# A fused cosine attention and mixer kernel: output of both heads in one tile, one pair transposed on TensorE, token and channel steps reordered

## The chip, the cores and the metric

The kernel runs on one core of one Trainium2 chip. The metric is device time in microseconds (us), the median over runs. The profile is one more execution of the same program; its times are counted from the start of its span.

## The reference

Eight batches, twelve heads, 448 positions, 64 columns a head. The attention normalizes the rows of q and k, divides the scores by tau = 0.1, and applies a softmax. Its output, heads side by side, is the input x of a mixer with a token product over positions and a channel product over columns:

```python
q_n = q / (norm(q) + 1e-06); k_n = k / (norm(k) + 1e-06)
attn = softmax(q_n @ k_n.T / tau)
x = (attn @ v)                      # [8, 448, 768]
h = relu(x.T @ w_tok1) @ w_tok2     # 448 -> 256 -> 448
u = x + h.T
out = u + relu(u @ w_ch1) @ w_ch2   # 768 -> 1536 -> 768
```

## The kernel before

**Pairs.** Two heads make a pair; six pairs make a batch, 48 pairs in all (i = 0 to 47). Work is written out pair by pair in an order fixed by hand: each engine executes its instructions in the order of the program, and waits on the others through semaphores. A "slot" is the stretch that begins with the scores of pair i and also does other steps of earlier and later pairs.

**Steps of a pair.** `load_qk` and `load_v` load it by DMA (issued by SP). `square` (L239 on ACT, L241 on POOL) and `sums` (L264, a reduction on VectorE) give the squared norms; `norms` turns them into factors by Ln and Exp on ACT (L277, L278) and a sum and a reciprocal on VectorE (L274, L275); `scale` (L293, mostly POOL) writes the normalized rows kq as fp16. They are then transposed into qk: by TensorE and a copy on VectorE (`tpose`, L317 and L319) for pairs below `DMA_T0` = 12, by a DMA transpose on SP (`tpose_dma`, L325) from there on. `score(i, c)` (L340) makes a piece of the transposed scores for both heads and ACT takes its exponential into pt (L341). There are four pieces in pairs 0 to 11; from pair 12 on (`old` is false) there are three and a rest (`score_rest`, L347), over 128 rows instead of 112. `pv(i, hh)` (L379) multiplies pt by v with a column of ones, for one head, and VectorE divides by that column (L382, L383), which gives x. `cast_v` is POOL's copy of v.

**Mixer.** `tok1` (L392) and its ReLU on VectorE (rt, L395), `tok2` (L406) and the addition that gives u (L409), both per pair. u is transposed into ut by DMA (`udma`, L415) or on TensorE (`upose`, L421). When a batch is whole, `refill` queues its channel work as units: `m_ch1` (psG, L431, ReLU on ACT L434), twelve a batch; `m_ch2` (psF, L446, addition L450), two of 384 columns for each block of 128 rows, with the output DMAs after the second. `unit` takes the next one from the queue, and `due` decides by a running account how many go into a slot.

**PSUM.** Two pools: `ps` (tag "b") with two tiles of one bank, `ps2` (tag "s") with three tiles of two banks. A new tile of a tag takes the buffer of the tile two (three) before it and waits until that has been read. In the slots of pairs 1 to 5 before the change, "b" goes in turn to the output of head 0, the transposes, the output of head 1 and `warm` (matmuls on the identity that keep TensorE busy, L331); "s" goes to two score pieces, tok1, two score pieces, tok2.

**Order.** Pairs 1 to 5 have one hand-written slot, pair 6 another, in one loop (L560 to L619). From pair 7 on the loop at L649 is used, with `side(i)` for the work on POOL, ACT and SP. After pair 47 the last token steps and the remaining units follow (L681 to L692).

Of the kernel before, what the change touches and what calls it, by code (L numbers as in the profile page):

```python
# [7 lines left out]
FP32 = mybir.dt.float32  # L8
FP16 = mybir.dt.float16
# [13 lines left out]
def kernel(  # L23
# [21 lines left out]
    CT = C // 128  # L45
    TT = T // 128
    DH = 384
    NDH = D // DH
    NPAIR = H // 2
    NP_ALL = B * NPAIR  # L50
    HP = 3
    NHALF = 2 * B
    inv_tau = 1.0 / float(tau)
    EPS_NORM = 1e-6
    DMA_T0 = 12
    OLD = 2 * NPAIR
    SINGLE = 3 * NPAIR

# [306 lines left out]
    def pv(i, hh):  # L365
# [10 lines left out]
        for m, lo in enumerate(windows(i // NPAIR)):  # L376
            for c in range(nch):
# [5 lines left out]
        nc.vector.tensor_tensor(out=st["x"][:, :, hh * E:(hh + 1) * E], in0=psO[:, :, 0:E],  # L383
                                in1=_bcast_free(rec[:], E), op=ALU.mult)

    def tok1(i, wide=False):
        st = pipe[i]
        w1 = (0, 1, 2, 3) if (i // NPAIR) % 2 == 0 else (4, 0, 1, 2)
        psR = (ps2 if wide else ps).tile([128, TT, 128], FP32, name=f"psR_{i}", tag="s" if wide else "b")
        for tt in range(TT):  # L390
            for m in range(4):
                nc.tensor.matmul(psR[:, tt], w1t[:, w1[m], tt * 128:(tt + 1) * 128], st["x"][:, m],  # L392
                                 start=(m == 0), stop=(m == 3))
        st["rt"] = att.tile([128, TT, 128], FP16, name=f"rt_{i}", tag="rt", bufs=2)
        nc.vector.tensor_scalar_max(out=st["rt"][:], in0=psR[:], scalar1=0.0)  # L395
# [39 lines left out]

    ost = {}

    def m_ch2(b, m, dh, wide):
        gt = gts[b // 2]
        lo = 384 if m == 3 else 128 * m + (b % 2) * 512  # L440
        if dh == 0:
            ost[0] = outp.tile([128, D], FP32, name=f"ost_{b}_{m}", tag="ost")
        o = ost[0]
        psF = (ps2 if wide else ps).tile([128, 512], FP32, name=f"psF_{b}_{m}_{dh}", tag="s" if wide else "b")
        for ct in range(CT):
            nc.tensor.matmul(psF[:, 0:DH], gt[:, ct, lo:lo + 128], wc2t[:, ct, dh * DH:(dh + 1) * DH],  # L446
                             start=(ct == 0), stop=(ct == CT - 1))

        def add(p0, p1, bb, slot):
            nc.vector.tensor_tensor(out=o[p0:p1, dh * DH:(dh + 1) * DH].rearrange("p (j e) -> p j e", j=3),  # L450
                                    in0=psF[p0:p1, 0:DH].rearrange("p (j e) -> p j e", j=3),
                                    in1=u16[bb][p0:p1, 3 * dh:3 * dh + 3, slot], op=ALU.add)

        if m < 3:
            add(0, 128, b, m + b % 2)
        else:
            add(0, 64, b - 1, 3)
            add(64, 128, b, 0)
        if dh == 0:
            return  # L460
        if m < 3:
            r = 0
            for c, p0, p1 in pieces(*MAIN[m]):
                nc.sync.dma_start(out=out[b].rearrange("(p c) d -> c p d", c=NCH)[c, p0:p1], in_=o[r:r + p1 - p0])
                r += p1 - p0
        else:
            (c, p0, p1), = pieces(384, S)
            for bb, r in ((b - 1, 0), (b, 64)):
                nc.sync.dma_start(out=out[bb].rearrange("(p c) d -> c p d", c=NCH)[c, p0:p1], in_=o[r:r + 64])

    def ns(cols, n=1):
        return n * (cols / 2.4 + 2.5)
# [2 lines left out]
        return [(ns(S, DT), lambda wide, ct=ct: m_ch1(b, ct, wide)) for ct in range(CT)]  # L475

    def ch2_units(b):
        return [(ns(DH, CT), lambda wide, m=m, dh=dh: m_ch2(b, m, dh, wide))
                for m in ((3, 0, 1, 2) if b == B - 1 else range(3 + b % 2)) for dh in range(NDH)]

    queue = []
    fed = [0.0, 0.0]
# [20 lines left out]
    with tc.manual_schedule():  # L503
# [53 lines left out]
        load_v(4)  # L557
        load_qk(6)

        for i in range(1, NPAIR + 1):  # L560
            b, pj = i // NPAIR, i % NPAIR
            if i < NPAIR:
                if i == 1:
                    scale(2, 0)
                    scale(2, 1, nc.vector)
                else:
                    scaled(i + 1)
                    if i != 3:
                        weights_ch1(max(i - 3, 0))
                load_qk(i + 6)  # L570
                score(i, 0)
                score(i, 1)
                sums(i + 2)
                norms(i + 2, i + 3)
                if i >= 2:
                    tok1(i - 2, wide=True)
                pv(i - 1, 0)
                norms(i + 2, i + 3, dve=True)
                cast_v(i)
                square(i + 3, 0)  # L580
                if i == 1:
                    warm(10)
                tpose(i + 1)
                score(i, 2)
                score(i, 3)
                if i >= 2:
                    tok2(i - 2, pe=True, wide=True)
                pv(i - 1, 1)
                warm(8)
                square(i + 3, 1, act=True)  # L590
                if i == 1:
                    place_w2()
                load_v(i + 4)
                if 2 <= i < NPAIR - 1:
                    udma(i - 2)
                continue
            load_qk(12)
            scaled(7)
            score(i, 0)
            score(i, 1)  # L600
            score(i, 2)
            sums(8)
            norms(8, 9)
            pv(i - 1, 0)
            pv(i - 1, 1)
            norms(8, 9, dve=True)
            cast_v(i)
            load_v(i + 4)
            squares(9)
            scaled(8)  # L610
            weights_ch1(3)
            upose(i - 3)
            tok1(i - 2, wide=True)
            score(i, 3)
            tpose(i + 1)
            tok2(i - 2, pe=True)
            tok1(i - 1, wide=True)
            tok2(i - 1, pe=True)
            sums(9)  # L619

# [26 lines left out]
        for i in range(NPAIR + 1, NP_ALL):  # L649
            b, pj = i // NPAIR, i % NPAIR  # L650
            for c in range(KC):
                score(i, c)
            pv_rest(i - 1)
            pv(i - 1, 0)
            pv(i - 1, 1)
            if i == NPAIR + 1:
                upose(NPAIR - 2)
                upose(NPAIR - 1)
                refill(0)
            elif pj == 2 and b > 1:  # L660
                refill(b - 1)
            side(i)
            fed[0] += fed[1]
            unit(True)
            if old(i):
                score(i, KC)
            else:
                score_rest(i)
            if i > NPAIR + 1:
                tok2(i - 2)  # L670
            if i + 1 < DMA_T0:
                tpose(i + 1)
            if due():
                unit(True)
            while due():
                unit()
            tok1(i - 1)
            if i + 2 < SINGLE:
                for t in SU_AT.get(i, [i + 3]):
                    sums(t)  # L680
        last = NP_ALL - 1  # L681
        pv_rest(last)
        pv(last, 0)
        pv(last, 1)
        tok2(last - 1)
        unit()
        tok1(last)
        unit()
        tok2(last)
        refill(B - 1)  # L690
        while queue:
# [36 lines left out]
```

## Time and profile before

| What | Value |
|---|---|
| median of 5 runs | 397.64 us (396.24 to 398.49) |
| the profiled execution | 397.75 us, its span 396.0 us |
| TensorE busy | 376.0 us (95%), granted clock 0.988 on average |
| ACT, POOL, DVE busy | 224.7, 236.1, 210.7 us |
| slots 2 to 5 (pairs 2 to 5), first score to first score | 4.60, 4.36, 4.30, 4.18 us |
| slot 6 | 6.82 us (37.22 to 44.04) |
| slot 12 | 8.40 us (78.33 to 86.73) |
| DMA of weights, wc2t, second half | issued at 66.5 us, lands 10.8 us later |
| last units of the loop to the last batch's channel stage | 342.86 to 361.59 us |

PE is TensorE's matmul stream and PEld its weight loads, DVE is VectorE, SP issues DMAs. A matmul's row ends later than the next one starts, because matmuls are pipelined; on the chain of work that ended last they are cut to what they add. The granted clock is the share of full speed that TensorE was allowed.

### The profile page before, as it was taken

The numbers are of one execution on the slowest core, as the hardware profiler recorded it, in microseconds if no ns is written. First come the engines' busy times: TensorE is split into PE (matmuls) and PEld (weight loads), VectorE is DVE, ScalarE is ACT, GpSimd is POOL, SyncE is SP. The second block draws the span as 40 slices with busy tenths as digits, with TensorE's granted clock in tenths as the row PEclk, the third lists the DMA queues.
The fourth block names the chain that finished last, engine by engine and source line by source line (L and its number), as shares of the span: only waits on it lengthen the run. The fifth ranks groups of instructions, "written<-read, shape, count | busy, mean of one in ns | idle before, by whom it ended". The sixth has DMA issues, their size and how long they took to land.

```text
span 396.0 us, 10211 instructions
## 1 busy us (share of the span) xinstructions
PE 376.0 (95%) x4132; PEld 243.4 (61%) x4132; DVE 210.7 (53%) x469; ACT 224.7 (57%) x378; POOL 236.1 (60%) x383
## 2 busy tenths in 40 slices
PE   5799799799999999999999999999999999999994
PEld 5567566466656666666666666667656666655562
DVE  6889767557545565366444574465544553331031
ACT  5899578655665456764684447764674546511400
POOL 6899887888779392948678492939585540000000
PEclk8999999989999999999999999999999999999998
DMA  8999999997896689876997788695796394023022
GB/s 206 243 232 213 235 266 193 217 228 174 166 228 147 175 204 216 159 164 148 195 209 165 165 213 215 139 181 120 203 204 130 75 174 68 15 56 91 0 81 81
DMA packets 117951, 65.26 MB, mean 165 GB/s; under 512 B 75920, under 2 KB 114320, under 8 KB 117904
## 3 DMA queue, kind: packets, MB, share of 16 engines
q1 hardware_dynamic: 113104, 58.71, 68.6%
q0 software_dynamic: 4080, 5.21, 7.6%
q10 hardware_dynamic: 720, 0.69, 0.7%
q8 instruction: 32, 0.52, 0.6%
q14 instruction: 15, 0.12, 0.1%
HBM read 43.45 MB, written 11.01 MB: 138 GB/s over the span
## 4 chain that ended last, share of the span: by engine, by line
PE 81%; ACT 4%; DMA 4%; DVE 4%; POOL 4%; issue 2%; POOLq 0%
PE psF L446 28%; PE psG L431 25%; PE psO L379 9%; PE psS L340 6%; PE psU L406 5%; PE psR L392 4%; ACT pt L341 3%; DMA w2n<-in_moe_w_tok_dram 2%; DMA qk<-kq 2%; PE psQ L347 2%; POOL kq L293 2%; PE psO L362 1%; DVE ssq L264 1%; POOL w1t L182 1%; DVE ost L450 1%
## 5 line engine op out<-in xcount | busy, mean ns | idle before, releaser
L341 ACT ACTIVATE pt<-psS 128x896 f16<-128x896 f32 (+1 forms) x156 | 132.5, 917 | 58.4 <-PE psS L340 58.0
L431 PE MATMUL psG<-ut,wc1t 128*128 128x448 f16 x576 | 116.8, 352 | 0.8 <-ACT gt L434 0.8
L446 PE MATMUL psF<-wc2t,gt 128*128 128x384 f16 x672 | 117.1, 328 | 0.2 <-ACT gt L434 0.2
L446 PEld LDWEIGHTS <-gt 128*128 128x128 f16 x672 | 64.0, 98 | 40.0 <-issue 1.7
L434 ACT ACTIVATE gt<-psG 128x448 f16<-128x448 f32 x96 | 51.3, 543 | 60.9 <-PE psG L431 60.9
L293 POOL TENSOR_TENSOR kq<-kf,rn 128x384 f16<-128x384 f32 (+1 forms) x47 | 42.3, 900 | 72.6 <-ACT rn L281 62.0
L431 PEld LDWEIGHTS <-wc1t 128*128 128x128 f16 x576 | 53.8, 98 | 45.4 <-issue 1.1
L450 DVE TENSOR_TENSOR ost<-psF,u 128x384 f32<-128x384 f32 (+1 forms) x64 | 35.5, 555 | 65.2 <-PE psF L446 63.8
L264 DVE TENSOR_REDUCE ssq<-sq 128x15 f32<-128x960 f32 (+2 forms) x49 | 55.7, 1140 | 3.2 <-ACT sq L239 3.1
L395 DVE TENSOR_SCALAR rt<-psR 128x256 f16<-128x256 f32 x48 | 20.2, 420 | 62.6 <-PE psR L392 62.5
L293 POOL TENSOR_TENSOR kq<-qf,rn 112x512 f16<-112x512 f32 x45 | 47.0, 1044 | 3.0
L379 PE MATMUL psO<-vt,pt 128*128 128x65 f16 (+1 forms) x1248 | 48.7, 194 | 0.0
L379 PEld LDWEIGHTS <-pt 128*128 128x128 f16 (+1 forms) x1248 | 42.6, 98 | 5.1 <-issue 1.9
L340 PE MATMUL psS<-qk 64*128 64x448 f16 x312 | 41.2, 358 | 3.6 <-DMA qk<-kq 2.4
L383 DVE TENSOR_TENSOR x<-psO,rec 128x256 f16<-128x256 f32 x96 | 40.8, 425 | 3.3
L241 POOL TENSOR_TENSOR sq<-kf 128x384 f32<-128x384 f32 (+1 forms) x46 | 40.1, 873 | 1.9 <-DVE ssq L264 1.8
L241 POOL TENSOR_TENSOR sq<-qf 112x512 f32<-112x512 f32 x39 | 40.5, 1039 | 0.0
L409 DVE TENSOR_TENSOR u<-psU,x 128x512 f16<-128x512 f32 x48 | 33.0, 687 | 6.0 <-PE psU L406 4.4
L382 DVE RECIPROCAL rec<-psO 128x4 f32<-128x4 f32 x96 | 16.9, 176 | 29.8 <-PE psO L379 29.8
L406 PEld LDWEIGHTS <-w2t 128*128 128x128 f16 x384 | 24.6, 98 | 10.5 <-issue 3.3
L406 PE MATMUL psU<-rt,w2t 128*128 128x128 f16 x384 | 29.4, 219 | 1.7 <-DVE rt L395 1.1
L348 ACT ACTIVATE pt<-psQ 128x448 f16<-128x448 f32 x36 | 19.4, 539 | 18.6 <-PE psQ L347 18.6
(55 smaller groups left out, 266.7 us busy)
## 6 DMA issues: line engine op xcount, KB each, us to landing
qf<-in_q_dram SPq DMA_DIRECT2D x48, 224.0 KB, 3.9
kf<-in_k_dram SPq DMA_DIRECT2D x36, 192.0 KB, 3.5
vf<-in_v_dram SPq DMA_DIRECT2D x36, 192.0 KB, 3.2
vf<-in_v_dram SPq DMA_DIRECT2D x12, 224.0 KB, 8.7
out_dram<-ost SPq DMA_DIRECT2D x8, 336.0 KB, 3.2
wc1t<-in_moe_w_ch_dram POOLq DMA_DIRECT2D x4, 576.0 KB, 10.6
wc2t<-in_moe_w_ch_dram POOLq DMA_DIRECT2D x2, 1152.0 KB, 11.5
out_dram<-ost SPq DMA_DIRECT2D x8, 288.0 KB, 3.0
```

Source lines behind the costliest of these rows:

```text
L241: nc.gpsimd.tensor_mul(out=dst, in0=src, in1=src)
L264: nc.vector.tensor_reduce(out=h["ssq"][0:n, col, sl], in_=pipe[i]["sq"][0:n, sl], axis=AXX.X, op=ALU.add)
L293: eng.tensor_tensor(out=kq[0:p, a, 0:n].rearrange("p c g e -> p g c e"), in0=st["kq"[a]][:].rearrange("p (g c) e -> p g c e", g=2), in1=_b ...
L340: nc.tensor.matmul(psS[:, hh, 0:S], qk[hb, c * n:c * n + 128], qm[hb], start=True, stop=True)
L341: nc.scalar.activation(out=pts[i % 2][0:n, 2 * S * c:2 * S * (c + 1)].rearrange("p (h s) -> p h s", h=2), in_=psS[0:n, :, 0:S], func=AF.Ex ...
L379: nc.tensor.matmul(psO[:, m, 0:E + 1], pts[i % 2][0:n, at:at + 128], vt[0:n, i % HP, nch * hh + c, 0:E + 1], start=(old(i) and c == 0), st ...
L383: nc.vector.tensor_tensor(out=st["x"][:, :, hh * E:(hh + 1) * E], in0=psO[:, :, 0:E], in1=_bcast_free(rec[:], E), op=ALU.mult)
L406: nc.tensor.matmul(psU[:, m], w2t[:, tt, lo:lo + 128], st["rt"][:, tt], start=(tt == 0), stop=(tt == TT - 1))
L431: nc.tensor.matmul(psG[:, 0:S], wc1t[:, dt, ct * 128:(ct + 1) * 128], ut[b][:, dt].rearrange("p m s -> p (m s)")[:, lo:lo + S], start=(dt ...
L434: nc.scalar.activation(out=gt[:, ct, (b % 2) * S:(b % 2 + 1) * S], in_=psG[:, 0:S], func=AF.Relu)
L446: nc.tensor.matmul(psF[:, 0:DH], gt[:, ct, lo:lo + 128], wc2t[:, ct, dh * DH:(dh + 1) * DH], start=(ct == 0), stop=(ct == CT - 1))
L450: nc.vector.tensor_tensor(out=o[p0:p1, dh * DH:(dh + 1) * DH].rearrange("p (j e) -> p j e", j=3), in0=psF[p0:p1, 0:DH].rearrange("p (j e) ...
```

## The change

1. A new `pv_wide(i)` replaces `pv(i, 0)` and `pv(i, 1)` for pairs 0 to 5. It writes both heads into one two-bank tile of `ps2` and normalizes them with one reciprocal and one product. It stands behind scores 0 and 1, in place of head 0's product there and head 1's behind tok2.
2. In slots 2 to 5, tok1 and tok2 use `ps`, and tok1 stands ahead of `sums` and `norms`.
3. Slot 6 gets the same order; its scores 2 and 3 stand behind the transposes of pair 7. Its second tok2 (pair 5) goes behind the first three score pieces of slot 7.
4. `DMA_T0` is 13: pair 12 is transposed by `tpose` in slot 11.
5. After the last pair, five channel units are placed ahead of and between its steps, where two were placed before.
6. The last block of rows (batch 7, m = 2) is computed in 384, 256 and 128 columns. Its first 640 columns are stored once they are done, its last 128 by two DMAs of which ACT issues one.

```diff
-    DMA_T0 = 12
+    DMA_T0 = 13
...
+    def pv_wide(i):
+        st = pipe[i]
+        vt = vts[(i // HP) % NV]
+        st["x"] = att.tile([128, 4, 128], FP16, name=f"x_{i}", tag="x", bufs=3)
+        psO = ps2.tile([128, 2, 512], FP32, name=f"psO_{i}", tag="s")
+        o = psO[:, :, 0:4 * (E + 2)].rearrange("p h (m e) -> p h m e", m=4)
+        for hh in range(2):
+            for m, lo in enumerate(windows(i // NPAIR)):
+                for c in range(NCH):
+                    at = (2 * c + hh) * S + lo
+                    nc.tensor.matmul(o[:, hh, m, 0:E + 1], pts[i % 2][0:SC, at:at + 128],
+                                     vt[0:SC, i % HP, NCH * hh + c, 0:E + 1], start=(c == 0), stop=(c == NCH - 1))
+        rec = att.tile([128, 2, 4], FP32, name=f"rec_{i}", tag="rec2", bufs=2)
+        nc.vector.reciprocal(out=rec[:], in_=o[:, :, :, E])
+        nc.vector.tensor_tensor(out=st["x"][:].rearrange("p m (h e) -> p h m e", h=2), in0=o[:, :, :, 0:E],
+                                in1=_bcast_free(rec[:], E), op=ALU.mult)
...
         if m < 3:
             r = 0
-            for c, p0, p1 in pieces(*MAIN[m]):
-                nc.sync.dma_start(out=out[b].rearrange("(p c) d -> c p d", c=NCH)[c, p0:p1], in_=o[r:r + p1 - p0])
+            for n, (c, p0, p1) in enumerate(pieces(*MAIN[m])):
+                eng = nc.scalar if st and n == 0 else nc.sync
+                eng.dma_start(out=out[b].rearrange("(p c) d -> c p d", c=NCH)[c, p0:p1, st:hi],
+                              in_=o[r:r + p1 - p0, st:hi])
                 r += p1 - p0
...
+        cuts = ((0, DH, None), (DH, D, 0))
+        ends = ((0, DH, None), (DH, D - 128, 0), (D - 128, D, D - 128))
...
-                score(i, 0)
-                score(i, 1)
-                sums(i + 2)
-                norms(i + 2, i + 3)
-                if i >= 2:
-                    tok1(i - 2, wide=True)
-                pv(i - 1, 0)
-                norms(i + 2, i + 3, dve=True)
...
-                if i >= 2:
-                    tok2(i - 2, pe=True, wide=True)
-                pv(i - 1, 1)
-                warm(8)
...
+            score(i, 0)
+            score(i, 1)
+            if i >= 2:
+                tok1(i - 2)
+            sums(i + 2)
+            norms(i + 2, i + 3)
+            pv_wide(i - 1)
+            norms(i + 2, i + 3, dve=True)
...
+            tpose(i + 1)
             score(i, 2)
+            score(i, 3)
+            if i >= 2:
+                tok2(i - 2, pe=True)
+            warm(8)
...
-            upose(i - 3)
-            tok1(i - 2, wide=True)
-            score(i, 3)
-            tpose(i + 1)
-            tok2(i - 2, pe=True)
-            tok1(i - 1, wide=True)
-            tok2(i - 1, pe=True)
-            sums(9)
+        upose(i - 3)
+        tpose(i + 1)
+        score(i, 2)
+        score(i, 3)
+        tok2(i - 2, pe=True)
+        tok1(i - 1)
+        sums(i + 3)
...
             for c in range(KC):
                 score(i, c)
+            if i == NPAIR + 1:
+                tok2(i - 2, pe=True)
             pv_rest(i - 1)
...
         last = NP_ALL - 1
+        unit()
         pv_rest(last)
         pv(last, 0)
         pv(last, 1)
+        unit(True)
         tok2(last - 1)
-        unit()
+        unit(True)
         tok1(last)
-        unit()
+        unit(True)
+        unit(True)
         tok2(last)
         refill(B - 1)
```

## The prediction

> **What bounds the kernel now.** I read the chain that ended last first: it is 81% TensorE, so time lost or won counts where TensorE stands still, or where another engine paces it. Then I took windows over the stages and the timelines of the four places that the diff touches. Below, "slot i" is the stretch that starts with the scores of pair i; its start is the first L340 matmul.
>
> From the page and the windows (columns: busy time and count of PE, PEld, DVE, ACT, POOL; granted clock; DMA share; GB/s):
>
> ```profile
> PE 81%; ACT 4%; DMA 4%; DVE 4%; POOL 4%; issue 2%; POOLq 0%
> 20.00:37.20 17.20, 16.43 (x288) 12.36 (x284) 15.44 (x39) 16.87 (x30) 17.20 (x21) 1.00 1.19 221
> 37.20:44.00 6.80, 5.08 (x86) 3.90 (x84) 5.38 (x15) 4.30 (x8) 6.75 (x8) 1.00 1.32 229
> 78.30:86.70 8.40, 8.37 (x79) 5.35 (x79) 3.21 (x9) 3.48 (x6) 8.04 (x15) 0.80 1.02 237
> ```
>
> Slots 2 to 5 (20 to 37.2) have four engines nearly full; slot 6 (37.2 to 44.0) has a TensorE that idles 1.7 us of 6.8; slot 12 (78.3 to 86.7) runs at a clock of 0.80.
>
> What paces slots 2 to 5 is in the timeline of slot 5:
>
> ```profile
> 33.67 1.22 DVE L264 TENSOR_REDUCE ssq<-sq 112x16 f32<-112x1024 f32 x1
> 34.81 0.42 DVE L395 TENSOR_SCALAR rt<-psR 128x256 f16<-128x256 f32 x1
> 35.05 0.32 ACT L277 ACTIVATE rn<-ssq,tiny 112x16 f32<-112x16 f32 x1
> 35.35 0.42 DVE L383 TENSOR_TENSOR x<-psO,rec 128x256 f16<-128x256 f32 x1
> 36.07 0.56 DVE L319 COPY qk<-pst 128x896 f16<-128x896 f16 x1
> 36.68 0.61 PE L331 MATMUL warm<-id 128*128 128x128 f16 x8
> 37.22 0.74 PE L340 MATMUL psS<-qk 64*128 64x448 f16 x6
> ```
>
> The filler matmuls (warm, L331) start 0.05 us after the copy of the transposed pair (L319) ends: their PSUM tile takes the one-bank buffer that this copy frees. The next scores stand behind them. So a loop paces the slot: copy, warm 0.54, scores, two exponentials 1.7, Ln and Exp (L277, L278), the norms on VectorE, copy: 4.18 us from 33.04 to 37.22.
>
> Pair 12, in the timeline:
>
> ```profile
> 70.59 1.23 SPq L325 DMA_TRANSPOSE qk<-kq  x1
> 78.33 0.74 PE L340 MATMUL psS<-qk 64*128 64x448 f16 x6 [2.38 <-DMA qk<-kq]
> 80.40 3.36 PE L446 MATMUL psF<-wc2t,gt 128*128 128x384 f16 x12
> 85.59 1.23 SPq L325 DMA_TRANSPOSE qk<-kq  x1
> ```
>
> The transpose by DMA takes 7.69 us, TensorE waits 2.38 us, and then twelve matmuls take 3.17 us on the chain where the others take 1.95.
>
> The end:
>
> ```profile
> 345.48 0.62 PE L406 MATMUL psU<-rt,w2t 128*128 128x128 f16 x8 [0.37 <-DVE x L383]
> 391.01 0.56 DVE L450 TENSOR_TENSOR ost<-psF,u 128x384 f32<-128x384 f32 x1 [1.39 <-PE psF L446]
> 391.60 0.79 SPq L464 DMA_DIRECT2D out_dram<-ost  x2
> ```
>
> [...] Here 2.38 us of waiting was enough for a mean of 0.80 over 8.4 us; the trace decides. [...] The trace agrees (VectorE's order above is the program's), and my largest cost rests on it. [...] The trace agrees from PSUM: 256 elements 0.42, 384 0.56, 512 0.69 us.
>
> **Part 1, slots 1 to 5: wide output tile.** VectorE trades two reciprocals of 0.17 and two products of 0.42 for one reciprocal (taken as 0.19) and one product of 512 elements (0.69, the u row L409). That saves 0.3 us of work a slot. No matmul is added. The output now takes the ring of three score tiles, five uses a slot in place of six; each use waits for the one three back. Scores 2 and 3 wait for the exponentials of scores 0 and 1, done at 1.3 and 2.2 us, when TensorE reaches them at 2.43; the output waits for score 3's exponential, which it reads anyway. I cost the ring at 0.
>
> The cost is the order. tok1 now stands before sums, so its ReLU (rt, L395) is queued on VectorE ahead of the reduction (L264), which ACT's Ln waits for. From a slot's start at 0: scores 0 and 1 take 0.49, tok1 0.45; rt starts 0.65 after tok1's start (57.32 to 57.97 in the trace), at 1.14, where the reduction began at 0.63 before. With the trace's start-to-start distances: rt 0.34, reduction 1.14 (ends near 2.70), reciprocal 0.20, product 0.62: norms at 3.44. ACT's Ln starts at 2.75, Exp ends at 3.33, so neither is later than VectorE itself. Norms 0.38, then the copy 3.82 to 4.38, warm at 4.43, the next scores at 4.97. Before: 4.18 to 4.60 a slot. Slot 1 has no tok1; its copy comes some 0.12 later. Slot 2 then starts at 19.90 and four slots of 4.97 put slot 6 at 39.78, not 37.22: **+2.56 us**. POOL needs at most 4.36 a slot and is no longer the pace. Bounds: 0, if the reduction finds VectorE as early as now; +3.2, if each of the four loses the full 0.79.
>
> **Part 2, slots 6 and 7.** Moved: scores 2 and 3 behind the transposes of pair 7; the second tok2 behind slot 7's scores; sums(9) on VectorE ahead of that tok2's addition. SP's and POOL's order is the same here, and no DMA is moved. From slot 6's start: copy of pair 7 ends 4.74, tok1(5) 4.80 to 5.25 (its buffer is freed by that copy), so slot 7 starts at 5.25, before 6.82. In slot 7: sums(9) holds VectorE from 5.64, u(5) is added 6.78 to 7.47, the second head's output waits for that buffer and starts at 7.53, x is done at 8.8, the two upose end at 9.07, and the first channel matmul follows; before 10.13 (47.35 less 37.22). **-1.06 us**; bounds -1.6 (the start of slot 7 passes on whole) and -0.3.
>
> **Part 3, pair 12 on TensorE.** Added in slot 11: eight transposes of 0.056 = 0.45 us of TensorE and a copy of 1024 columns (0.61 x 1024/896 = 0.69), at 75.10 to 75.79 in the shadow of a channel unit. Slot 12 can start at 75.79+0.45 = 76.24, not 78.33: -2.09. The clock then stays up: slot 12 sums to 0.67+1.12+1.95+0.19+0.45+1.95+0.45 = 6.78, before 8.40: -1.62. SP loses 1.23 us of issue and its wait for POOL (66.1 to 70.6), so the loads of pairs 17 and 18 go earlier.
>
> What is late next is pair 14. POOL runs without a gap from kq(13) (ends 77.45) over two pairs' squares (4.13), the casts (0.84) and kq(14) (2.9): 85.27, whatever TensorE does. Its transposes take 3.1 to 4.1 us (4.1 at 79.2 and 85.6), so they land at 88.4 to 89.4. TensorE would want them at 76.24+6.78+4.70 = 87.72. I take a wait of 1.3. It is shorter than the one that lowered the clock, so I add no slow stretch. Pair 13 is ready at 77.5+4.1 = 81.6 and wanted at 83.0; pair 15 has more room. Net **-2.4**; bounds -3.7 (no wait) and -1.0 (a wait of 1.3 that lowers the clock as well).
>
> **Part 4, after the last pair.** The same units in another order. Before, from the loop's end at 342.86 to 361.59, TensorE stood 2.0 us. After: the first unit waits for a buffer until 343.66; the second head's output waits for its ReLU (343.66+1.94 = 345.60). Then without a wait: output 1.06, unit 1.14, tok2 0.45, unit 1.95, tok1 0.45, two units 3.90, tok2 0.45, three units 5.85: 360.85. **-0.74**; bounds -1.5 and -0.2. The transposed u of the last pair is issued at 355.9 and lands 2.4 later; it is wanted at 361.8.
>
> **Part 5, the last row block.** 256 and 128 columns for 384: TensorE 1.31+0.67 for 1.95; [...] ACT issues one piece, but SP is still issuing the two wide pieces until 391.6, so its last goes out then, not at 391.99: **-0.4**; bounds 0 and -0.9.
>
> **The sum**: +2.56 -1.06 -2.4 -0.74 -0.4 = -2.04. The profiled execution took 397.75 (span 396.0 and 1.75 around it), 0.1 above the median of the five runs, 397.64. So 395.7, and 395.6 against the median.
>
> **The rivals.** (a) The first slots cost nothing, rt being done in VectorE's gaps: parts 2 to 5 alone give 393.0. For: VectorE idles 0.3 before each reduction now. Against: the order in its queue. Chance 0.22. (b) Slower: pair 14's transposes land late, as pair 12's did (7.7 us), now that the loads of pairs 17 and 18 crowd forward. Slot 14 starts at 85.3+7.7 = 93.0, the clock drops once more (+1.6), 3.2 later than before (91.43); with +1.5 of parts 1 and 2 and -1.14 of the end, 401.2. It decides from a latency of some 5.4 us on: 85.3+5.4+1.6 is 0.85 past 91.43, which with +1.5 and -1.14 makes 1.2. For: DMA moves 237 GB/s here. Against: the 7.7 ran beside a weight load of 1152 KB (66.5 to 77.3), and no such load follows. Chance 0.10. (c) Parts 2 and 3 give only their small ends, since the weights of the second product come later under the earlier loads: about 397.6, chance 0.18. (d) My sum: 0.50. That the change is not what it says I rule out: each part is read off the order.
>
> **Numbers.** Likeliest 395.6. A difference of 0.3% (1.2 us) is about what a measurement of this kernel can tell from none: faster is below 396.4. Most of (d) (0.40 of 0.50) and all of (a): 0.62. Same: the rest of (d) and most of (c): 0.24. Slower: 0.14. Range 392.5 to 398.6: from just past (a) to (c)'s slow side; it leaves out (b).
>
> **What would show it.** Right: four slots of nearly 5 us before slot 6, the L264 reduction following rt; slot 12 within 6 us of slot 11 and at full clock; a DMA wait of about 1 us at pair 14; 18 us from the loop's last unit to the last batch's channel stage. Wrong: slots still of 4.2 us (then 393), a wait at pair 13, or a dip of the clock near 85 to 95.

## The result, and the profile after

The changed kernel takes 394.87 us (median of 44 runs; 393.85 to 400.1), the kernel before 397.65 us in its runs beside it: a ratio of 0.9943, with a 95% interval of 0.9927 to 0.9959. By the medians it is faster by 2.8 us, by the ratio by 2.3 (interval 1.6 to 2.9); 2.0 were forecast. The ratios leave out the few runs that are over 1.5% above the fastest of their kernel; the medians leave them out only where it is said.

The profiled execution of the changed kernel took 394.40 us, its span 392.6; before it was 397.75 and 396.0. Line numbers have moved: scores L339, filler L330, transposes on TensorE L316 and their copy L318, transposes by DMA L324, ReLU of the token product L412, the wide output L396 and its product L400, u L426, channel products L448 and L464.

From the page after, the chain by engine, and the clock in 40 slices:

```profile
PE 82%; DVE 8%; POOL 3%; DMA 2%; issue 2%; ACT 1%; SPq 0%; POOLq 0%
```

```profile
PEclk9899999999999999999999999999999999999999
```

VectorE's share of the chain doubled, 4% to 8%: in slots 2 to 5 TensorE now waits for it. DMA's fell from 4% to 2%, and no slice after the second has a clock under 9.

The span cut at the same landmarks in both traces, in us (psG is the first product of the channel stage):

| Stretch | before | after | difference |
|---|---|---|---|
| start to slot 1 (nothing was changed there) | 15.44 | 15.13 | -0.31 |
| slot 1 | 4.34 | 3.93 | -0.41 |
| slots 2 to 5 | 17.44 | 19.94 | +2.50 |
| slot 6 to the first psG | 10.13 | 9.33 | -0.80 |
| first psG to slot 11 | 23.17 | 23.16 | 0 |
| slot 11 to slot 14 | 20.91 | 17.99 | -2.92 |
| slot 14 to the loop's end | 251.43 | 251.45 | 0 |
| loop's end to the last batch's psG | 18.73 | 17.86 | -0.87 |
| from there to the end | 34.41 | 33.81 | -0.60 |

The rows add up to -3.4, the difference of the spans. The two stretches between the changed places differ by 0.02 at most.

**Slot 5**, timeline after (columns: start, length, engine, line, operation, and in brackets the idle time before it and what ended it):

```profile
35.16 0.42 DVE L412 TENSOR_SCALAR rt<-psR 128x256 f16<-128x256 f32 x1 [1.14 <-PE psR L409]
...
35.50 1.21 DVE L263 TENSOR_REDUCE ssq<-sq 112x16 f32<-112x1024 f32 x1
...
36.74 0.31 ACT L276 ACTIVATE rn<-ssq,tiny 112x16 f32<-112x16 f32 x1 [0.60 <-DVE ssq L263]
36.86 0.69 DVE L400 TENSOR_TENSOR x<-psO,rec 128x512 f16<-128x512 f32 x1
...
37.84 0.56 DVE L318 COPY qk<-pst 128x896 f16<-128x896 f16 x1
38.46 0.61 PE L330 MATMUL warm<-id 128*128 128x128 f16 x8 [0.89 <-DVE qk L318]
39.00 0.55 PE L339 MATMUL psS<-qk 64*128 64x448 f16 x4
```

VectorE idles 1.14 us until it gets the token product; the reduction (ssq) stands behind rt in VectorE's queue and follows at once. ACT then idles 0.60 for the reduction, and TensorE 0.89 for the copy. Slots 2 to 5 took 4.99, 4.98, 4.99 and 4.98 us.

**Slots 6 and 7**, timeline after:

```profile
43.24 0.61 PE L423 MATMUL psU<-rt,w2t 128*128 128x128 f16 x8 [1.02 <-DVE ut L439]
...
46.69 0.67 PE L378 MATMUL psO<-vt,pt 112*128 112x65 f16 x16 [0.57 <-DVE u L426]
...
48.33 1.30 PE L448 MATMUL psG<-ut,wc1t 128*128 128x448 f16 x6
```

Slot 6 fell from 6.82 to 5.31 us. In slot 7 the output of the second head waits 0.57 for u(5), whose tok2 was moved there, and gives part of that back.

**Pairs 12 to 14**, timeline after:

```profile
75.18 0.61 PE L316 MATMUL pst<-id,kq 128*128 128x128 f16 x8
...
77.30 0.74 PE L339 MATMUL psS<-qk 64*128 64x448 f16 x6
...
78.45 1.81 SPq L324 DMA_TRANSPOSE qk<-kq  x1
...
79.01 2.12 PE L464 MATMUL psF<-wc2t,gt 128*128 128x384 f16 x12
...
84.80 0.74 PE L339 MATMUL psS<-qk 64*128 64x448 f16 x6 [0.65 <-DMA qk<-kq]
...
86.12 1.23 SPq L324 DMA_TRANSPOSE qk<-kq  x1
...
89.48 0.74 PE L339 MATMUL psS<-qk 64*128 64x448 f16 x6
```

and windows over slots 11 (from 71.5) and 12 (from 77.3), with the columns of the prediction's windows:

```profile
71.50:77.30 5.80, 5.80 (x78) 3.75 (x77) 4.24 (x10) 4.71 (x9) 4.22 (x9) 1.00 1.18 185
77.30:84.80 7.50, 6.85 (x81) 4.61 (x80) 5.23 (x13) 3.69 (x7) 7.25 (x13) 1.00 1.11 248
```

Pair 12 waits for nothing, the clock is 1.00 in slot 12, and its twelve matmuls of psF take 2.12 us in place of 3.36. The DMA wait that is left is 0.65 us, at pair 13; there is none at pair 14.

**The end**, timeline after:

```profile
340.93 0.61 PE L409 MATMUL psR<-x,w1t 128*128 128x128 f16 x8
...
341.72 1.29 PE L448 MATMUL psG<-ut,wc1t 128*128 128x448 f16 x6 [0.18 <-ACT gt L451]
...
343.65 0.28 PE L361 MATMUL psO<-vt,pt 64*128 64x65 f16 x7 [0.50 <-ACT gt L451]
...
358.79 13.78 PE L448 MATMUL psG<-ut,wc1t 128*128 128x448 f16 x72
...
388.24 0.29 DVE L468 TENSOR_TENSOR ost<-psF,u 128x128 f32<-128x128 f32 x1 [0.25 <-PE psF L464]
388.56 0.35 ACTq L483 DMA_DIRECT2D out_dram<-ost  x1
```

The loop ends with the token product at 340.93. Two waits are left behind it, 0.18 ahead of the first unit and 0.50 ahead of the second head's output; the last addition takes 0.29 in place of 0.56.

### The profile page after: what moved, and what is told of

It is laid out like the page before. It is cut to its first block, busy times and chain, and to the rows that moved or that the text cites. A ratio compares the mean times of both kernels' runs of the same rounds, so it can differ in the third digit from the quotient of the medians.

```text
span 392.6 us, 10246 instructions
## 1 busy us (share of the span) xinstructions
PE 374.5 (95%) x4152; PEld 243.9 (62%) x4152; DVE 209.6 (53%) x459; ACT 225.2 (57%) x378; POOL 236.1 (60%) x383
## 3 DMA queue, kind: packets, MB, share of 16 engines
q0 software_dynamic: 4080, 5.21, 7.7%
## 4 chain that ended last, share of the span: by engine, by line
PE 82%; DVE 8%; POOL 3%; DMA 2%; issue 2%; ACT 1%; SPq 0%; POOLq 0%
PE psG L448 26%; PE psF L464 26%; PE psO L378 9%; PE psS L339 7%; PE psR L409 5%; PE psU L423 5%; DVE ssq L263 3%; DMA qk<-kq 2%; PE psQ L346 2%; PE psO L361 1%; POOL w1t L181 1%; DVE x L400 1%; DVE ost L468 1%; POOL kq L292 1%; DVE qk L318 1%
## 5 line engine op out<-in xcount | busy, mean ns | idle before, releaser
L448 PE MATMUL psG<-ut,wc1t 128*128 128x448 f16 x576 | 116.8, 352 | 0.8 <-ACT gt L451 0.8
L464 PE MATMUL psF<-wc2t,gt 128*128 128x384 f16 (+2 forms) x684 | 116.2, 323 | 0.0
L464 PEld LDWEIGHTS <-gt 128*128 128x128 f16 x684 | 64.2, 98 | 38.1
L448 PEld LDWEIGHTS <-wc1t 128*128 128x128 f16 x576 | 53.9, 98 | 45.3 <-issue 1.1
L468 DVE TENSOR_TENSOR ost<-psF,u 128x384 f32<-128x384 f32 (+2 forms) x65 | 35.7, 549 | 62.8 <-PE psF L464 60.2
L412 DVE TENSOR_SCALAR rt<-psR 128x256 f16<-128x256 f32 x48 | 20.2, 421 | 67.2 <-PE psR L409 67.1
L339 PE MATMUL psS<-qk 64*128 64x448 f16 x312 | 41.1, 358 | 2.3 <-DVE ost L468 0.9
L378 PE MATMUL psO<-vt,pt 128*128 128x65 f16 (+1 forms) x1056 | 40.5, 194 | 0.6 <-DVE u L426 0.6
L378 PEld LDWEIGHTS <-pt 128*128 128x128 f16 (+1 forms) x1056 | 35.4, 97 | 4.3 <-issue 1.4
L382 DVE TENSOR_TENSOR x<-psO,rec 128x256 f16<-128x256 f32 x84 | 35.7, 425 | 2.9
L426 DVE TENSOR_TENSOR u<-psU,x 128x512 f16<-128x512 f32 x48 | 33.0, 687 | 4.4 <-PE psU L423 2.8
L381 DVE RECIPROCAL rec<-psO 128x4 f32<-128x4 f32 x84 | 14.8, 177 | 29.5 <-PE psO L378 29.5
L409 PEld LDWEIGHTS <-w1t 128*128 128x128 f16 x384 | 25.0, 98 | 8.4 <-issue 1.9
```

The lines of the kernel that those rows point to most:

```text
L339: nc.tensor.matmul(psS[:, hh, 0:S], qk[hb, c * n:c * n + 128], qm[hb], start=True, stop=True)
L378: nc.tensor.matmul(psO[:, m, 0:E + 1], pts[i % 2][0:n, at:at + 128], vt[0:n, i % HP, nch * hh + c, 0:E + 1], start=(old(i) and c == 0), st ...
L448: nc.tensor.matmul(psG[:, 0:S], wc1t[:, dt, ct * 128:(ct + 1) * 128], ut[b][:, dt].rearrange("p m s -> p (m s)")[:, lo:lo + S], start=(dt ...
L464: nc.tensor.matmul(psF[:, 0:hi - lo], gt[:, ct, at:at + 128], wc2t[:, ct, lo:hi], start=(ct == 0), stop=(ct == CT - 1))
L468: nc.vector.tensor_tensor(out=o[p0:p1, lo:hi].rearrange("p (j e) -> p j e", e=128), in0=psF[p0:p1, 0:hi - lo].rearrange("p (j e) -> p j e" ...
```

## The experiments

Each ratio is to the kernel before on the same chip, with its 95% interval; the changed kernel itself stands at 0.9943.

### Which part carries the gain

Pair 12 alone, in the kernel before:

```diff
-    DMA_T0 = 12
+    DMA_T0 = 13
```

> The kernel before with DMA_T0 = 13 alone: pair 12 is transposed on TensorE, nothing else is changed. Theory A (part 3 of the prediction, as corrected by the profile after): slot 12 starts 5.8 us after slot 11 instead of 7.8, the clock stays at 1.0 over slot 12, a wait of 0.5 to 1.3 us at pair 13 or 14 remains; slot 14 starts 2.4 to 3.0 us earlier than before, the kernel takes 394.6 to 395.2, as much as the whole change. Rival E (pair 12's gain in the changed kernel depended on its later arrival after longer first slots): pairs 13 or 14 wait 2 us or more for the transpose by DMA, the clock falls there, and the gain is under 1 us.

Measured: 394.66 us, ratio 0.9927 (0.9906 to 0.9948). One line gives as much as the whole change. Slot 11's start to slot 14's is 18.06 us (before 20.91). Window over slot 12 and a line of the timeline:

```profile
75.70:83.20 7.50, 6.82 (x80) 4.59 (x79) 5.26 (x13) 3.66 (x7) 7.27 (x13) 1.00 1.12 239
```

```profile
83.23 0.74 PE L340 MATMUL psS<-qk 64*128 64x448 f16 x6 [0.71 <-DMA qk<-kq]
```

The clock is whole, and the small wait at pair 13 is here too, so it comes from this line and not from the new slots.

Parts 1 and 2 alone, in the kernel before: the loop of slots 1 to 5, slot 6 and the moved tok2 from the changed kernel, the rest as before.

```diff
-        for i in range(1, NPAIR + 1):
+        for i in range(1, NPAIR):
...
-                score(i, 0)
-                score(i, 1)
-                sums(i + 2)
-                norms(i + 2, i + 3)
-                if i >= 2:
-                    tok1(i - 2, wide=True)
-                pv(i - 1, 0)
...
+            if i >= 2:
+                tok1(i - 2)
+            sums(i + 2)
+            norms(i + 2, i + 3)
+            pv_wide(i - 1)
...
```

> The kernel before with parts 1 and 2 of the change alone: wide output tile, order of slots 1 to 6, last tok2 of batch 0 behind slot 7's scores; pair 12, the steps after the last pair and the last row block as before. Theory A: slots 2 to 5 are 4.98 us, slot 1 0.4 shorter, slot 6 and the first half of slot 7 0.8 shorter; the first channel matmul starts 1.0 to 1.5 us later than before and pair 12 still waits 2.4 us, so the kernel is slower, 398.7 to 399.1. Rival F (the time lost is given back at pair 12, because the transposes there land at a moment that the weight load sets and not TensorE): the wait at pair 12 shrinks to about 1 us and the time is 397.4 to 397.9.

Measured: 399.0 us, ratio 1.0019 (0.9986 to 1.0052): on the slow side, but the interval holds no change. In the trace the slots take 4.98 us and the first psG starts 0.99 later than before. The profiled execution was nevertheless not slower (397.4 us), and the timeline at pair 12 says why:

```profile
71.59 1.32 SPq L325 DMA_TRANSPOSE qk<-kq  x1
...
78.89 0.74 PE L340 MATMUL psS<-qk 64*128 64x448 f16 x6 [1.95 <-DMA qk<-kq]
```

The transposes were issued 1.00 us later than before, about as much as TensorE was late, but they landed after 7.3 us in place of 7.7. So the wait shrank from 2.38 to 1.95; the clock was 1.00 in the slot after it, and that slot took 6.78 in place of 8.40. In this execution a slightly shorter transfer, and the clock that stayed up, paid for the slots. Over all 14 runs that is not so: the median lies 1.3 us above that of the kernel before (397.66), which is about the loss of the slots themselves.

Parts 4 and 5 alone, in the kernel before:

```diff
+        unit()
         pv_rest(last)
         pv(last, 0)
         pv(last, 1)
+        unit(True)
         tok2(last - 1)
-        unit()
+        unit(True)
...
+        ends = ((0, DH, None), (DH, D - 128, 0), (D - 128, D, D - 128))
```

> The kernel before with parts 4 and 5 of the change alone: channel units between the last pair's steps, and the last row block in three pieces with one store issued by ACT. Theory A: from the end of the loop's last unit to the last batch's channel stage 17.9 us (18.7 before), from there to the end of the span 33.8 (34.4 before): 1.4 us off the time, 396.2 to 396.4, with everything ahead of the last pair, pair 12's wait of 2.4 us too, as before. Rival J (part of what the changed kernel gains there comes from the earlier arrival of the last pairs): less than 0.8 us.

Measured: 396.63 us, ratio 0.9973 (0.9948 to 0.9999). In the trace the tail is 0.87 shorter and the last stage 0.77. These 1.64 us are 0.4% of the time, which the interval holds, on the side of the larger gain.

Pair 12 is as before in this kernel, and its trace gives one more length of the wait there:

```profile
77.93 0.74 PE L339 MATMUL psS<-qk 64*128 64x448 f16 x6 [2.20 <-DMA qk<-kq]
```

After it the clock is 0.79 from 77.9 to 86.2, and the slot takes 8.32 us.

### What made slots 2 to 5 longer

The prediction blames the order in VectorE's queue. In slots 2 to 6 of the changed kernel, the reduction ahead of the token product:

```diff
+            sums(i + 2)
             if i >= 2:
                 tok1(i - 2)
-            sums(i + 2)
```

> The changed kernel with one edit: in slots 2 to 6 the reduction sums (L263) is written ahead of tok1, so it stands ahead of the ReLU rt on VectorE, while TensorE's order stays. Theory A (VectorE's queue order made slots 2 to 5 longer, 4.98 us each after the change): the reduction starts 0.6 us after the slot's first score instead of 1.5, ACT's Ln no longer waits for it, and a slot falls to 4.4 to 4.5 us; the kernel is about 2 us faster than the changed one, near 392.9. Rival B (the wide tile itself does it: its single product of 0.69 us, or its place in the ring of score tiles): slots stay at 4.9 or more and the time within 0.5 us of 394.9.

Measured: 394.96 us, ratio 0.9935 (0.9908 to 0.9963). Slots 3 to 5 fall to 4.55 each and slot 6 from 5.31 to 4.87. Slot 2 rises from 4.99 to 5.21: there the reduction waits 1.43 us for a square on ACT (L238). The first psG comes 1.55 earlier; the median does not follow, a miss. Timeline of slot 5, then of TensorE at pairs 13 and 14:

```profile
33.99 1.22 DVE L263 TENSOR_REDUCE ssq<-sq 112x16 f32<-112x1024 f32 x1 [0.65 <-ACT sq L238]
...
35.13 0.41 DVE L412 TENSOR_SCALAR rt<-psR 128x256 f16<-128x256 f32 x1
...
35.74 0.69 DVE L400 TENSOR_TENSOR x<-psO,rec 128x512 f16<-128x512 f32 x1
...
36.73 0.56 DVE L318 COPY qk<-pst 128x896 f16<-128x896 f16 x1
...
37.35 0.61 PE L330 MATMUL warm<-id 128*128 128x128 f16 x8 [0.45 <-DVE qk L318]
```

```profile
85.46 0.74 PE L339 MATMUL psS<-qk 64*128 64x448 f16 x6 [2.86 <-DMA qk<-kq]
...
87.03 3.77 PE L464 MATMUL psF<-wc2t,gt 128*128 128x384 f16 x12
```

```profile
85.40:91.80 6.40, 6.34 (x67) 3.97 (x67) 2.44 (x8) 3.49 (x6) 3.82 (x9) 0.73 0.98 219
```

The reduction now runs before rt, and the slot is 0.43 shorter. It is still 0.37 longer than slot 5 before (4.18). Most of that is the wide product: from its start to the start of the copy are 0.99 us (35.74 to 36.73), where the product of one head left 0.72 (35.35 to 36.07 in the prediction's lines). So the order is the larger cause, and the second head's output ahead of the copy the smaller.

At pair 13 TensorE waits 2.86 us for the transposes in place of 0.65 (+2.2), and the clock falls to 0.73 over 6.40 us (6.40 x 0.27 = 1.7, an estimate of what that cost). -1.55 + 2.2 + 1.7 = +2.35 on the profiled 394.40 makes 396.75; that execution took 396.78. What held the transposes back is in the queues of POOL and SP:

```profile
69.90 4.86 SPq L432 DMA_TRANSPOSE ut<-u  x1
...
75.83 1.04 POOL L292 TENSOR_TENSOR kq<-qf,rn 112x512 f16<-112x512 f32 x1
...
80.01 1.27 SPq L324 DMA_TRANSPOSE qk<-kq  x1
```

Pair 13's rows were ready 1.55 us earlier, as TensorE was (76.87 for 78.42). SP issued their transposes only 3.1 us after that: the issue of an earlier DMA had held its queue for 4.86 us, and the loads of pairs 17 and 18, which stand between the two, were issued that much later. In the changed kernel's trace that one issue took 1.19. Why it took so long is not shown, and it need not be so in every execution: 5 of the 19 runs are faster than the fastest of the changed kernel's 44 (393.85), down to 392.60.

The filler still waited for the copy. Without it in slots 2 to 5 of the changed kernel, the order left as it is:

```diff
-            warm(8)
+            else:
+                warm(8)
```

> The changed kernel without the eight filler matmuls (warm) in slots 2 to 5; slot 1 keeps them. Theory A (the loop that paces a slot runs through the copy of the transposed pair, the filler behind it and then the next scores): the next scores start 0.05 us after the copy, a slot is shorter by the filler's 0.49 to 0.54 us (4.98 to about 4.5), together about 2 us, near 393.0. Rival C (the filler is needed, TensorE's clock falls without it): granted clock below 1.0 somewhere in 19 to 40 us and matmuls at double distance, time 394.9 or more. Rival D (the filler only fills idle time that ACT or VectorE sets): slots stay at 4.98.

Measured: 394.83 us (394.35 over the runs that the ratio takes), ratio 0.9924 (0.9899 to 0.9948). Timeline, two slots on end, in an execution whose slot 1 began 2.0 us late:

```profile
35.79 0.55 PE L339 MATMUL psS<-qk 64*128 64x448 f16 x4 [0.90 <-DVE qk L318]
...
40.24 0.55 PE L339 MATMUL psS<-qk 64*128 64x448 f16 x4 [0.90 <-DVE qk L318]
```

The scores wait for the copy themselves, 0.54 earlier than behind the filler, and slots 3 to 5 are 4.45 us each (slot 2 4.70). The clock stays at 1.00 in slots 2 to 6, so the filler was not needed for it there. It stood on this loop before the change too, so it is no cause of the longer slots, only time that they could do without. Against the changed kernel the gain is not clear, since the intervals overlap; but 9 of the 22 runs are below 393.85, the fastest of the changed kernel's 44.

The moved tok2 of slot 6, put back into slot 6, in one run:

```diff
         tok1(i - 1)
+        tok2(i - 1, pe=True)
         sums(i + 3)
...
-            if i == NPAIR + 1:
-                tok2(i - 2, pe=True)
```

> The changed kernel with the last tok2 of batch 0 back at the end of slot 6, ahead of sums(9) (one look, to read slots 6 and 7). Theory A (what the move saves is TensorE's wait for the ReLU): slot 7 starts 6.4 to 6.6 us after slot 6 and not 5.3, the wait of 0.57 us for u(5) goes, and the first channel matmul comes 9.9 to 10.1 us after slot 6's start and not 9.33. Rival L (the move gives nothing, since VectorE's reduction holds the outputs back in both): 9.2 to 9.5.

Measured in the trace (398.05 us in a run whose slot 1 began 2.0 us late): slot 6 takes 6.51 us, and the first psG starts 9.82 after it, against 9.33.

```profile
48.16 0.61 PE L423 MATMUL psU<-rt,w2t 128*128 128x128 f16 x8 [0.59 <-DVE rt L412]
```

In its old place the product waits for its own ReLU. The move is worth 0.49 of part 2's 0.80.

### What the wait at pair 12 cost, and what sets the landing of the transposes

Filler in the kernel before, at the end of slot 11, so that TensorE is busy for most of the wait:

```diff
             tok1(i - 1)
+            if i + 1 == DMA_T0:
+                warm(38)
```

> The kernel before with 38 filler matmuls (2.1 us) at the end of slot 11, in the time in which TensorE waits for pair 12's transposes by DMA; nothing else is changed, the transposes stay on DMA. Theory A (the idle wait of 2.4 us is what lowers the clock): slot 12 still starts about 8 us after slot 11, but lasts 6.8 us and not 8.4, the clock stays at 1.0 around 79 to 87 us, and the kernel is about 1.6 us faster than before in a run of the profiled kind (near 396.0). Rival G (the clock falls for another reason, or the slow matmuls of slot 12 wait for weights): slot 12 still lasts 8.4 us with filler in front of it, time as before.

Measured: 396.97 us, ratio 0.9984 (0.9957 to 1.001). Timeline, and a window over slot 12:

```profile
75.46 2.29 PE L331 MATMUL warm<-id 128*128 128x128 f16 x38
...
78.76 0.74 PE L340 MATMUL psS<-qk 64*128 64x448 f16 x6 [1.01 <-DMA qk<-kq]
```

```profile
78.70:85.50 6.80, 6.74 (x79) 4.57 (x79) 3.08 (x9) 3.49 (x6) 5.68 (x11) 1.00 1.20 239
```

Slot 12 falls from 8.40 to 6.78 us at a clock of 1.00, though it starts later than before and the DMA beside it moves as much (239 GB/s, before 237): the 1.62 were the price of standing idle, not of the traffic. That execution keeps little of it, and the time shows no gain, a miss: pair 12's transposes took 8.4 us here, pair 14 waits 0.39, and from slot 11's start to slot 14's are 20.50 us (before 20.91).

The loads of pairs 17 and 18 behind pair 13's transposes, in the changed kernel:

```diff
+            def loads():
                 for t in range(i + n, i + (8 if i == 2 * NPAIR - 1 else n + 1)):
...
                 if i + 2 >= DMA_T0:
                     tpose_dma(i + 2)
+            if i == 2 * NPAIR - 1:
+                loads()
```

> The changed kernel with one edit: the loads of pairs 17 and 18 (slot 11) are issued behind pair 13's transposes by DMA and not ahead of them. Theory H (transfers are served in order: pair 13's transposes landed 2.2 us behind the last of these loads, all of them behind the weight load that landed at 79.3): the transposes land by 82 us instead of 84.8, the wait of 0.65 us at pair 13 is gone, pair 14 may wait up to 0.7 for its own; median 394.0 to 394.6, and fewer runs near 398. Rival I (the weight load itself keeps the transposes back): they still take 6 us, the wait stays, the time stays at 394.9.

Measured: 399.71 us, ratio 1.0051 (1.0027 to 1.0076): slower, a miss. Pair 13's transposes landed after 4.9 us in place of 6.3 and nothing waited for them, as it would be if the loads had been in their way. Timeline at pair 14, and a window over its slot:

```profile
78.51 1.23 SPq L324 DMA_TRANSPOSE qk<-kq  x1
...
86.13 1.24 SPq L432 DMA_TRANSPOSE ut<-u  x1
...
88.59 1.24 SPq L324 DMA_TRANSPOSE qk<-kq  x1
...
92.71 1.30 PE L339 MATMUL psS<-qk 64*128 64x448 f16 x6 [3.80 <-DMA qk<-kq]
```

```profile
92.70:101.00 8.30, 8.29 (x69) 5.14 (x70) 2.87 (x8) 3.49 (x6) 5.78 (x9) 0.65 1.05 236
```

SP issues one DMA after another here. From 78.5 to 89.9 us its queue was full: the six moved loads held it from 79.8 to 84.1, v, the transposed u and the next loads followed, and the transposes of pair 14 were issued at 88.59, though their rows were ready at 86.1 and the changed kernel issues them at 86.12. TensorE then waited 3.80, and the clock fell to 0.65. By estimate that costs 3.80 - 0.65 + 8.30 x 0.35 = 6.1; the profiled execution was 5.8 longer (400.18). This is the mechanism of the prediction's slower rival (b), called up by a queue in place of a latency.

### Versions meant to beat both

Four edits at once on the changed kernel: sums first, no filler, the loads late, and sums(9) behind u(5) in slot 7.

```diff
             if i == NPAIR + 1:
                 tok2(i - 2, pe=True)
+                sums(i + 2)
```

> The changed kernel with four edits: sums ahead of tok1 in slots 2 to 6, no filler in slots 2 to 5, sums(9) behind the addition of u(5) in slot 7, and the loads of pairs 17 and 18 behind pair 13's transposes. Theory A with H: slots 2 to 5 take 4.2 to 4.4 us (ACT and POOL pace them again), the wait of 0.57 us for u(5) is gone, the first channel matmul comes 2.5 to 3 us earlier than in the changed kernel; pair 13 does not wait, pair 14 waits about 1 us. The kernel takes 392.2 to 392.8. Rival I (the DMA stretch between 67 and 90 us is a gate that the first slots cannot move): pairs 13 or 14 wait 2.5 us or more, with a lower clock behind it in part of the runs, time 394 to 395.

Measured: 397.47 us, ratio 0.9994 (0.9972 to 1.0016), a miss. The slots came down to between 4.2 and 4.7 us, but the late loads made pair 14 wait 3.81 us again. The fourth edit was wrong as well:

```profile
46.07 0.94 PE L438 MATMUL psT<-id,u 128*128 128x128 f16 x8 [1.01 <-DVE x L382]
```

The wait for u(5) shrank from 0.57 to 0.27, but the one for x, which now stands behind the reduction, grew from 0.46 to 1.01.

A second pair on TensorE instead, so that pair 13 needs no DMA either, with sums first:

```diff
-    DMA_T0 = 13
+    DMA_T0 = 14
```

> The changed kernel with sums ahead of tok1 in slots 2 to 6 and DMA_T0 = 14, so that pair 13 too is transposed on TensorE (0.45 us more of TensorE, one transpose less on DMA). Theory H: the 2.9 us wait at pair 13 and the lower clock after it, which the kernel with sums first alone showed, are gone; slots 2 to 5 stay at 4.55 us; slot 14 starts 1.0 to 1.5 us earlier than in the changed kernel and the time is 393.5 to 394.0, with runs above 397 rare. Rival I: the wait moves on to pair 14 at 2 us or more and the time stays near 394.9.

Measured: 394.23 us, ratio 0.9893 (0.9846 to 0.9941), over six runs. No DMA wait at pairs 12 to 14 is left, slot 11's start to slot 14's is 17.77 us, slots 3 to 5 take 4.55, and the first psG comes 31.67 us after slot 1's start (33.20 in the changed kernel): in this execution what sums first wins is kept. It is the shortest of the profiled ones, 392.31 us, and also the fastest of its six; the interval overlaps the changed kernel's.

The same without the filler:

> The changed kernel with three edits: sums ahead of tok1 in slots 2 to 6, no filler in slots 2 to 5, DMA_T0 = 14 (pairs 12 and 13 transposed on TensorE). Theory A with H: slots 2 to 5 take 4.2 to 4.4 us, the first channel matmul comes 31 us after slot 1's start (33.2 in the changed kernel), no wait for a transpose by DMA at pairs 12 and 13 and none over 0.7 us at pair 14. Span 389.5 to 390.5 in a run of the profiled kind, median 392.5 to 393.7. Rival I (the DMA stretch is a gate): a wait of 1.5 us or more for pair 14, span and median as with sums first and DMA_T0 = 14 (390.5, 394.2) or worse.

Measured: 392.48 us over the five runs that the ratio takes (392.04 to 394.03), 393.09 with the sixth; ratio 0.9874 (0.9838 to 0.9909), the lowest here. The interval lies below the changed kernel's own (0.9927 to 0.9959), though the two were not run on one chip; against the kernel with the filler it overlaps. The sixth, the profiled one, had a mean granted clock of 0.850 (434.3 us), so its timeline can't be laid beside the others.

The second pair on TensorE alone, on the changed kernel:

> The changed kernel with DMA_T0 = 14 alone; first slots as in the changed kernel (4.98 us). Theory H: the wait at pair 13 (0.65 us) goes, 0.45 us of TensorE comes; slot 14 starts 0 to 0.3 us earlier than in the changed kernel, the time is 394.5 to 394.9, and runs above 397 become rare, since no late transpose can let the clock fall. Rival K (the runs above 397 come from elsewhere): as many of them as in the changed kernel, a quarter of its runs.

Measured: 394.64 us, ratio 0.9939 (0.9914 to 0.9965). Slot 14 starts 0.24 earlier than in the changed kernel. Two of 15 runs lie above 397 us, of the changed kernel's 11 of 44: too few to say whether late transposes make its longer runs. A late start can make a run long: in the traces of "no filler" and of the moved tok2 slot 1 began 2.0 us late and slot 2 some 3 us late, and for the latter (398.05 us) that and its 0.49 are nearly all of the distance to the changed kernel's 394.40. How many of the longer runs start late stays open.

## Why the prediction was right, and where its steps were not

**Part 1: +2.56 forecast, +2.09 measured.** The four slots of 4.97 were 4.98 to 4.99, and the order inside is the one worked out: VectorE took rt (35.16) and then the reduction (35.50), as the program has them, and with sums first the reduction (33.99) and then rt (35.13). In slot 5 rt starts 1.14 after the slot's start, the norms 3.45 (3.44 forecast), the copy 3.82. Rival (a), slots at no cost, is out. The text of the prediction calls the order the cost; its sum also holds the longer product, and rightly: sums first takes 0.43 off slots 3 to 5, and most of the other 0.37 of slot 5 is that product. The term that failed is slot 1, +0.12 against -0.41: with only three uses of the one-bank ring there, the filler takes a buffer that is already free and runs ahead (it starts at 18.18, right behind the scores), so the scores of slot 2 wait 0.27 for the copy alone.

**Part 2: -1.06 forecast, -0.80 measured.** Slot 6 came out at 5.31 for 5.25. From its start the first psG comes after 9.33, not 9.07: besides slot 6's 0.06, the waits for u(5) and x in slot 7 are some 0.2 longer than worked out.

**Part 3: -2.4 forecast, -2.92 measured.** Slot 11 took 5.81 for 5.72, slot 12 without its wait 6.85 for 6.78, slot 13 4.68 for 4.70. The step that failed is "ready at 77.5+4.1 = 81.6" for pair 13: its latency was 6.3 us, not 4.1. The loads of pairs 17 and 18 ahead of it landed at about 82.6, the second half of wc2t at 79.3. With the loads moved it was 4.9; but in the two executions that started late it was 4.3 and 4.4 with the loads ahead, so how much either of them costs is not settled. The wait of 1.3 that I put at pair 14 was one of 0.65 at pair 13, and pair 14's transposes took 3.1 us and made none. The mechanism was named; place and size were off, in opposite senses, and a wait at pair 13 was one of the prediction's own signs of being wrong. Not so either is that POOL gets to kq(14) "whatever TensorE does": it was done there at 86.1, not 85.27. POOL begins kq(13) 4.03 us after slot 11's start before the change, after it and with sums first (74.55, 75.52 and 73.97 us), so it moves with TensorE. The bound of -1.0 is not what its terms give (-2.4 + 1.6 = -0.8); nothing hung on it. That the wait's own price is the clock, which I took from one window of 0.80, is shown by the filler in the wait. That pair 12 is the bulk of the gain is shown by its run alone.

**Parts 4 and 5: -1.14 forecast, -1.47 measured.** The tail gave -0.87 for -0.74, the last block -0.60 for -0.4; in the run of both alone -0.87 and -0.77. The last addition, of 128 elements, took 0.29 us, where the traces' 0.42 for 256 and 0.56 for 384 give an estimate of 0.28. The waits of the tail came as worked out: counted from the loop's end, the first unit starts after 0.79 (0.80 forecast) and the second head's output after 2.72 (2.74).

**The sum** was -2.04, the trace has -3.4, of which 0.31 lie in a start that was not touched, and the medians differ by 2.8. So the forecast was 0.7 too slow by the medians, for the reasons of slot 1, of pair 13's smaller wait, and of the end; part 2 is the one term that erred the other way. It is 0.2 too slow by the ratio, whose interval holds 2.0. That the number came so near is in part luck: three of the four terms were 0.3 to 0.5 short of the gain in the trace, and the runs gave less than the trace.

**Do the parts add?** The medians of the three runs with parts alone differ from the kernel before by -3.0, +1.3 and -0.9, together -2.6, and the whole by -2.8: on that they add. Single executions differ. Up to pair 14, what TensorE wins or loses can end in a wait for a transpose by DMA, which hangs on SP's queue and on the transfer's latency: with the slots alone the wait at pair 12 was 1.95 us in place of 2.38 and the clock stayed at 1.00, and with sums first one long issue on SP took back what the slots had won. The prediction has no term for this spread.

## What to carry to other kernels

Ahead of a step that is moved forward on one engine, look at what it puts behind itself on the others: a reduction of 1.2 us that stood behind a ReLU cost 0.4 us a slot, and the second head's product ahead of the copy another 0.3. Filler on the critical loop is not free either: here it cost 0.5 us a slot, and without it the clock stayed at 1.00 in slots 2 to 6. Before speeding up a stage, find the next transfer that TensorE will wait for. Sums first won nothing in the median alone (394.96 to 394.87), and a gain over the changed kernel is clear only with it, without the filler, and with pairs 12 and 13 off the DMA. Count every issue in the queue of the engine that issues DMAs; six loads moved behind one transpose delayed the issue of the next one by 2.5 us. And read one trace as one execution: beside it stand the other runs, which may say something else.

## What the runs showed of the hardware

**One wait can cost the clock.** Single waits of 2.20 (parts 4 and 5 alone), 2.38 (the kernel before), 2.86 (sums first) and 3.80 us (loads late) were followed by a clock of 0.79, 0.80, 0.73 and 0.65, and waits of 1.01 (filler in the wait) and 1.95 (slots alone) by none below 1.00. The mean of 0.80 in the kernel before holds a stretch at 0.50, from 80.4 to 82.4 us. The slot behind was longer by 1.5 to 2.5 us, some two thirds of the wait. The length of one wait is not all of it: at the start of the execution without filler, waits of 1.31 and 0.95, ending 1.7 us apart, were followed by 0.66 from 17 to 22 us (from the start of the output's 32 matmuls to the row behind them were 1.76 us there, 1.02 in the next slot). So the prediction's step from the wait of 2.38 us to an unharmed clock at 1.3 was an estimate from one case. What else decides, these few waits don't say.

**The latency of one DMA transpose of a pair** was 7.7 us for pair 12 in the kernel before, 7.3 with the slots alone and 8.4 with the filler in the wait, beside the weight load of 1152 KB (66.5 to 77.3 us in the kernel before). For pair 13 it was 4.1 before, 6.3 in the changed kernel, 6.4 with pair 12 alone, 5.4 with sums first and 4.9 with the loads late; for pairs 14 and 15, 4.1 and 3.1 before, 3.1 and 4.4 in the changed kernel. SP was busy 1.23 to 2.59 us with the issue of one in the kernel before (to 2.42 in the changed kernel), 1.19 (changed kernel) to 4.86 (sums first) with that of a transpose of u in slots 10 and 11, and up to 2.44 with that of a load in the timeline of slot 5 of the changed kernel.
